# Moving two hidden-layer sums ahead of two output additions on VectorE, in six of nine blocks

## The chip, the cores and the metric

The kernel runs on one core of a Trainium2 chip. A core has a matrix engine (TensorE, PE in the profile, with its weight loads shown as PEld), a vector engine (VectorE, DVE), a scalar engine (ScalarE, ACT), a general engine (GpSimd, POOL) and a queue processor (SyncE, SP) that issues DMAs. Each engine works through its own list of instructions in order; between engines, an instruction waits on semaphores. The metric is the device time of one execution in microseconds (us), lower is better.

## What is computed

The inputs are `q`, `k`, `v` of 8 batches, 8 heads, 576 rows and 64 columns, and the weights of a two-layer network. First comes an attention in which keys and values are averaged over groups of 8 rows (72 groups), then a residual network with a mixing over rows:

```python
attn = softmax(q @ mean8(k).T / sqrt(64));  x = attn @ mean8(v)   # heads side by side: 576 x 512
u  = x + lam * (w_tok @ (alpha1 * x + beta1))                     # mixing over rows
a2 = alpha2 * u + beta2
out = u + lam * (relu(a2 @ w_ch1) @ w_ch2)                        # 512 -> 2048 -> 512
```

## The kernel before, in words

The 8 x 576 rows are cut into 36 chunks of 128 rows, and four chunks make a block, so there are nine blocks (`NBLK`), n = 0 to 8. While TensorE computes the network of block n, the attention and the row mixing of batch b = n + 1 are woven in between. The last two blocks (n = 7 and 8) have no attention beside them.

The order of the work is written out by hand. For each block, a list `todo` of pairs (place, function) is filled and sorted by place (lines 934 to 1009), and the functions are called in that order; each engine gets its own instructions in the order of the calls. A place is a number between about 0 and 31 and only orders; it is no time.

The parts that matter here, with their places in a block n = 2 to 6:

- `mlp_A(n, j)` (L651): 4 matmuls per j into a PSUM tile `ps_h` (L662), then ScalarE writes the relu as bf16 (L669) into `H4[n, j // 4]`. Sixteen j, at places 0 to 15. Each `H4` tile holds four j and 512 columns (rows of the block): the "top" columns 0 to 255 and the "low" columns 256 to 511.
- `att_AV(b, h)` (L546): five small matmuls of the attention of one head (L556, L560), then on VectorE a reciprocal (L562) and a multiplication into `x_tm` (L564). Heads 4 to 7 are at 16.5, 17.0, 18.2 and 18.7.
- `att_X` (L574) with `rest_X` (L567): two products (L578 and L571) that write `xs`, the input of the mixing. For heads 4 and 5 they are on GpSimd (17.1), for heads 6 and 7 on VectorE (18.8).
- `mix_T(b, c)` (L607): five matmuls (L614; ten half-width ones for c = 4, which exists only for odd b) at 21.0 + 1.15 c (1.3 c for b = 2), then an addition on VectorE (L618) and a cast on ScalarE (L622); 1.8 places later a DMA (L633) transposes the result into `u_fm` for the first layer of a later block.
- From the third block on (`n >= FIRST`) the second layer is done by seven products of half size instead of eight (a Strassen-like scheme). `product(n, i, pp)` (L748) is product i for half pp: 8 matmuls of 256 columns (L775). The places are 16 + 2s + pp, with i in the order 1, 2, 4, 5, 6, 3, 7. Here they are called P1 to P7.
- `hidden_sum(n, i, g)` (L734, the instruction is L744): the sums over first-layer outputs which that scheme needs, on VectorE, in bf16, 128 x 1024. g = 0 takes `H4[n, 0]` and `H4[n, 2]`, g = 1 takes `H4[n, 1]` and `H4[n, 3]`: the first and the second half of the outputs. Sum 1 adds the low columns of `hi` to those of `lo` in place; P5 reads the result, in its first four matmuls that of g = 0 and in its last four that of g = 1. Sum 2 subtracts the top columns from that and writes `S2`, which P6 and sum 4 read. Sum 4 is read by P3.
- `gather(n, i)` (L779, the instruction is L793): the output additions. It adds a finished product from PSUM to `u_sb`, on VectorE. The first waits for P1, the second for P2. P1, P6 and P7 accumulate into the same PSUM bank (called V), with additions in between; so P6 may not begin before the first addition has read V.

```python
when = ((3, (4.6, 14.6)), (1, (8.6, 19.2)), (2, (8.8, 19.4)), (4, (22.3, 23.0)))   # L965: sum i, places of g = 0, 1
order = (1, 2, 5, 6, 4, 7, 3) if last else (1, 2, 4, 5, 6, 3, 7)                   # L971
todo.append((16 + 2 * s + pp, lambda i=i, pp=pp: product(n, i, pp)))               # L974
todo.append((17.05 + 2 * s + (1.9 if i == 1 and not last else 0) + 0.01 * part,    # L976
             lambda i=i, part=part: gather(n, i, part)))
1: (lo[:, :, low], lo[:, :, low], hi[:, :, low], ALU.add),                         # L740: out, in0, in1, operation
2: (S2, lo[:, :, low], lo[:, :, top], ALU.subtract),                               # L741
nc.vector.tensor_tensor(out=o, in0=o, in1=banks[key, "both"], op=ALU.add)          # L793
```

The first output addition stands at 17.05 + 1.9 = 18.95, the second at 17.05 + 2 = 19.05. So VectorE's list in blocks n = 2 to 6 is: head 7 (L562, L564), the two products for `xs` (L578, L571), output addition 1, output addition 2, sum 1 of the second half, sum 2 of the second half, the addition of mixing 0 (L618), output addition 4 (21.05), and so on. In block n = 7 it is the same without attention and mixing. The last block (n = 8) has places of its own (L967).

Of the kernel before, what the change touches and what calls it, by code (L numbers as in the profile page):

```python
# [23 lines left out]
def kernel(  # L24
# [668 lines left out]
    def store(n, m, c0=0, c1=DM, queues=(nc.sync, nc.sync)):  # L693

        b, c = chunks[4 * n + m]
        u = u_of[n][:, m, c0:c1]
        if c < 4:
            queues[0].dma_start(
                out=out[b, 0:512, :].rearrange("(p c) d -> p c d", c=4)[:, c, c0:c1], in_=u)
        else:  # L700
            for i in range(2):
                queues[i].dma_start(out=out[b + i, 512:576, c0:c1], in_=u[64 * i:64 * i + 64, :])
# [31 lines left out]
    def hidden_sum(n, i, g):  # L734

        lo, hi, S2, S3 = H4[n, g], H4[n, g + 2], wino["S2"][g], wino["S3"][g]
        top, low = slice(0, HALF), slice(HALF, DM)
        o, a, b, op = {
            3: (S3, lo[:, :, top], lo[:, :, low], ALU.subtract),
            1: (lo[:, :, low], lo[:, :, low], hi[:, :, low], ALU.add),  # L740
            2: (S2, lo[:, :, low], lo[:, :, top], ALU.subtract),  # L741
            4: (lo[:, :, top], hi[:, :, top], S2, ALU.subtract),
        }[i]
        nc.vector.tensor_tensor(out=o, in0=a, in1=b, op=op)  # L744
# [3 lines left out]
    def product(n, i, pp):  # L748

        def stat(j):  # L750
            g, r = j // 4, j % 4
            t = {6: wino["S2"][g], 7: wino["S3"][g]}.get(i, H4[n, g + 2 * (i in (2, 4))])
            c0 = (HALF if i in (4, 5) else 0) + 128 * pp
            return t[:, r, c0:c0 + 128]

        def moving(j):
            g, r = j // 4, j % 4
            return {1: w2[g][:, r, 0:HALF], 2: w2[g + 2][:, r, 0:HALF],
                    3: w2[g + 2][:, r, HALF:], 4: w2[g][:, r, HALF:],
                    5: wino["T1"][:, j], 6: wino["T2"][g][:, r], 7: wino["T3"][:, j]}[i]  # L760

        last = n == NBLK - 1
        key = {1: "V", 6: "V", 7: "V", 2: "X", 4: "Y", 5: "Z", 3: "Z"}[i]
        first = i in (1, 2, 4, 5)
        if first and pp == 0:
            tile = (psB.tile([P, DM], FP, tag="ch", bufs=2, name="ps_w") if i < 3
                    else gp("ps_w")).rearrange("p (a d) -> p a d", a=2)
            banks[key] = [tile[:, 0], tile[:, 1]]
            banks[key, "both"] = tile
        alone = last and i == 5  # L770
        if alone and pp:
            banks[key][1] = gp("ps_w").rearrange("p (a d) -> p a d", a=2)[:, 1]
        ps = banks[key][pp]
        for j in range(8):
            nc.tensor.matmul(out=ps, lhsT=stat(j), rhs=moving(j), stop=(j == 7),  # L775
                             start=(first and (pp == 0 or alone) and j == 0),
                             skip_group_check=True)

    def gather(n, i, part=0):  # L779

        U = u_of[n]
        top, low = slice(0, 2), slice(2, 4)
        L, R = slice(0, HALF), slice(HALF, DM)
        rows, cols = {1: ((top, L),), 2: ((top, L),), 4: ((low, L),), 5: ((low, R),),
                      6: ((top, R),), 3: ((top, R),), 7: ((low, L), (low, R))}[i][part]
        key = {1: "V", 6: "V", 7: "V", 2: "X", 4: "Y", 5: "Z", 3: "Z"}[i]
        if key == "Z" and n == NBLK - 1:
            for pp in range(2):
                o = U[:, rows.start + pp, cols]
                nc.vector.tensor_tensor(out=o, in0=o, in1=banks[key][pp], op=ALU.add)  # L790
            return
        o = U[:, rows, cols]
        nc.vector.tensor_tensor(out=o, in0=o, in1=banks[key, "both"], op=ALU.add)  # L793
# [140 lines left out]
    for n in range(NBLK):  # L934
# [27 lines left out]
                todo.append((1.2 + g, lambda g=g: weight_sum(4, g)))  # L962
        if n >= FIRST:
            last = n == NBLK - 1
            when = ((3, (4.6, 14.6)), (1, (8.6, 19.2)), (2, (8.8, 19.4)), (4, (22.3, 23.0)))  # L965
            if last:
                when = ((3, (4.6, 12.6)), (1, (8.6, 16.1)), (2, (8.8, 16.2)), (4, (18.6, 19.6)))  # L967
            for i, at in when:
                for g in range(2):
                    todo.append((at[g], lambda i=i, g=g: hidden_sum(n, i, g)))  # L970
            order = (1, 2, 5, 6, 4, 7, 3) if last else (1, 2, 4, 5, 6, 3, 7)  # L971
            for s, i in enumerate(order):
                for pp in range(2):
                    todo.append((16 + 2 * s + pp, lambda i=i, pp=pp: product(n, i, pp)))  # L974
                for part in range(2 if i == 7 else 1):
                    todo.append((17.05 + 2 * s + (1.9 if i == 1 and not last else 0) + 0.01 * part,  # L976
                                 lambda i=i, part=part: gather(n, i, part)))
            if last:
                for m in range(2):
                    todo.append((19.1, lambda m=m: store(n, m, 0, HALF)))  # L980
                    todo.append((28.1, lambda m=m: store(n, 2 + m, queues=(nc.sync, nc.scalar))))
                    todo.append((29.2, lambda m=m: store(
                        n, m, HALF, DM, ((nc.sync, nc.scalar)[m],) * 2)))
            else:
                for m in range(4):
                    todo.append((27.2 if m < 2 else 29.2, lambda m=m: store(n, m)))
# [53 lines left out]
```

## Time and profile before

| | us |
|---|---|
| device time, three runs | 341.84, 343.35, 344.87 |
| their median | 343.35 |
| span of the profiled execution, first to last instruction | 339.7 |
| PE busy in that span | 328.1 (97%) |
| DVE, ACT, POOL busy | 237.3, 175.4, 94.5 |
| block n = 2 in the trace (109.0 to 144.4) | 35.4 |
| block n = 3 (144.4 to 178.3) | 33.9 |
| block n = 7 (283.0 to 309.1) | 26.1 |

For the profiled execution the page gives its span, 339.7 us, and no other time; the three runs are 2.1 to 5.2 us longer than that, the median 3.65 us. The blocks n = 2, 4, 6 have the ten half-width matmuls of a fifth mixing and are longer by 1.5 us than n = 3 and 5. Times within the trace are in us from the start of the span. Busy time of PE is not the same as PE at its peak, since matmuls overlap in the records: a 256-column matmul is listed with 0.273 us, while eight of them in a row begin 0.87 us apart from the next group, or 0.109 us each.

### The profile page before, as it was taken

The numbers are of one execution on the slowest core, as the hardware profiler recorded it, in microseconds if no ns is written. First come the engines' busy times: TensorE is split into PE (matmuls) and PEld (weight loads), VectorE is DVE, ScalarE is ACT, GpSimd is POOL, SyncE is SP. The second block draws the span as 40 slices with busy tenths as digits, with TensorE's granted clock in tenths as the row PEclk, the third lists the DMA queues.
The fourth block names the chain that finished last, engine by engine and source line by source line (L and its number), as shares of the span: only waits on it lengthen the run. The fifth ranks groups of instructions, "written<-read, shape, count | busy, mean of one in ns | idle before, by whom it ended". The sixth has DMA issues, their size and how long they took to land.

```text
span 339.7 us, 6491 instructions
## 1 busy us (share of the span) xinstructions
PE 328.1 (97%) x2524; PEld 209.0 (62%) x2524; DVE 237.3 (70%) x486; ACT 175.4 (52%) x322; POOL 94.5 (28%) x110
## 2 busy tenths in 40 slices
PE   8999999979999999999999999999999999999994
PEld 3768754435444567755775576657765766586583
DVE  7672378699779979687868787786778783263263
ACT  3767989247611880279127913583258325704800
POOL 8869352611029002710162026201420200000000
PEclk9999999998999999999999999999999999999998
DMA  8999989951996994399539943896350035003003
GB/s 123 199 212 266 268 152 267 209 132 38 159 242 116 189 168 127 70 212 181 168 69 206 198 141 68 185 188 190 49 148 2 0 53 149 0 2 125 0 31 95
DMA packets 66168, 45.81 MB, mean 135 GB/s; under 512 B 34349, under 2 KB 56501, under 8 KB 66138
## 3 DMA queue, kind: packets, MB, share of 16 engines
q1 hardware_dynamic: 51788, 32.60, 41.8%
q0 software_dynamic: 13824, 12.40, 22.5%
q10 hardware_dynamic: 526, 0.40, 0.5%
q8 instruction: 20, 0.33, 0.4%
q14 instruction: 10, 0.08, 0.1%
HBM read 38.30 MB, written 9.44 MB: 141 GB/s over the span
## 4 chain that ended last, share of the span: by engine, by line
PE 78%; DVE 15%; DMA 4%; issue 2%; POOL 0%; DVEq 0%
PE ps_h L662 30%; PE ps_w L775 21%; PE ps_tok L614 9%; PE ps_ch L682 7%; DMA v_main<-in_v_dram 4%; DVE w L710 4%; PE ps_av L556 2%; DVE u_sb L793 2%; PE ps_s L513 2%; DVE x_tm L564 2%; PE ps_warm L605 1%; DVE xs L578 1%; DVE v_u L483 1%; DVE H L744 1%; PE ps_kp L445 1%
## 5 line engine op out<-in xcount | busy, mean ns | idle before, releaser
L662 PE MATMUL ps_h<-u_fm,w 128*128 128x512 bf16 (+2 forms) x608 | 135.5, 372 | 1.3 <-DVE u_sb L689 1.0
L669 ACT ACTIVATE H<-ps_h,bias_cols 128x512 bf16<-128x512 f32 x144 | 98.1, 688 | 60.2 <-PE ps_h L662 59.2
L662 PEld LDWEIGHTS <-w 128*128 128x128 bf16 x608 | 65.8, 114 | 52.3 <-issue 5.8
L775 PEld LDWEIGHTS <-H 128*128 128x128 bf16 x560 | 53.0, 98 | 13.3 <-DVE H L744 2.6
L622 ACT CAST u_bf<-u_sb 128x512 bf16<-128x512 f32 x32 | 19.8, 618 | 73.2 <-issue 41.5
L775 PE MATMUL ps_w<-w,H 128*128 128x256 bf16 x448 | 53.8, 273 | 0.0
L793 DVE TENSOR_TENSOR u_sb<-u_sb,ps_w 128x512 f32<-128x512 f32 x54 | 36.4, 685 | 21.7 <-PE ps_w L775 21.1
L578 POOL TENSOR_TENSOR xs<-x_tm,lamal_bc 128x512 bf16<-128x512 f32 x12 | 15.1, 1266 | 110.5 <-DVE x_tm L564 110.3
L614 PE MATMUL ps_tok<-xs,wtT 128*128 128x512 bf16 (+3 forms) x200 | 44.9, 380 | 0.0
L618 DVE TENSOR_TENSOR u_sb<-x_tm,ps_tok 128x512 f32<-128x512 f32 (+1 forms) x40 | 27.4, 685 | 13.4 <-PE ps_tok L614 13.3
L564 DVE TENSOR_TENSOR x_tm<-ps_av,rec 128x320 f32<-128x320 f32 x64 | 31.5, 492 | 2.7
L542 ACT ACTIVATE ET<-ps_s 72x512 f16<-72x512 f32 x56 | 32.3, 591 | 0.0
L682 PE MATMUL ps_ch<-w,H 128*128 128x512 bf16 x128 | 30.4, 379 | 0.0
L614 PEld LDWEIGHTS <-wtT 128*128 128x128 bf16 (+3 forms) x200 | 17.4, 100 | 16.0 <-issue 1.1
L562 DVE RECIPROCAL rec<-ps_av 128x5 f32<-128x5 f32 x64 | 12.2, 191 | 17.0 <-PE ps_av L560 16.7
L483 DVE TENSOR_TENSOR v_u<-v_u 72x1024 f32<-72x1024 f32 (+1 forms) x24 | 22.8, 948 | 0.2
L775 PE MATMUL ps_w<-w_t,h_s 128*128 128x256 bf16 x168 | 22.6, 273 | 0.0
L682 PEld LDWEIGHTS <-H 128*128 128x128 bf16 x128 | 11.9, 98 | 13.7 <-issue 0.4
L185 POOL TENSOR_TENSOR k_raw<-k_raw 128x512 f32<-128x512 f32 x14 | 19.2, 1368 | 0.0
L187 POOL TENSOR_TENSOR k_bf<-k_raw 128x512 bf16<-128x512 f32 x14 | 18.8, 1342 | 1.1
L775 PEld LDWEIGHTS <-h_s 128*128 128x128 bf16 x168 | 16.4, 98 | 4.1
L744 DVE TENSOR_TENSOR h_s<-H 128x1024 bf16<-128x1024 bf16 x21 | 14.5, 690 | 6.3 <-ACT H L669 5.8
(148 smaller groups left out, 349.8 us busy)
## 6 DMA issues: line engine op xcount, KB each, us to landing
out_dram<-u_sb SPq DMA_DIRECT2D x30, 256.0 KB
k_raw<-in_k_dram SPq DMA_DIRECT2D x12, 512.0 KB
v_u<-in_v_dram SPq DMA_DIRECT2D x12, 512.0 KB
q_bf<-in_q_dram POOLq DMA_DIRECT2D x16, 256.0 KB, 6.7
w<-in_moe_w_ch_dram POOLq DMA_DIRECT2D x6, 512.0 KB, 14.2
out_dram<-u_sb SPq DMA_DIRECT2D x10, 128.0 KB
w<-in_moe_w_ch_dram POOLq DMA_DIRECT2D x1, 1024.0 KB, 14.2
k_raw<-in_k_dram POOLq DMA_DIRECT2D x2, 512.0 KB, 17.5
```

Of the source, the lines that this page charges most:

```text
L185: eng.tensor_tensor(out=raw[:, :, 0:2], in0=raw[:, :, 0:2], in1=raw[:, :, 2:4], op=ALU.add)
L483: nc.vector.tensor_tensor(out=out, in0=t[:, :, 0:width], in1=t[:, :, width:2 * width], op=ALU.add)
L542: nc.scalar.activation(out=o, in_=i, func=AF.Exp, bias=0.0, scale=0.125)
L564: nc.vector.tensor_tensor(out=x[:, 1 - odd:6 - odd, dd:dd + D], in0=av[:, :, 0:64], in1=rec.unsqueeze(2).to_broadcast((P, 5, D)), op=ALU.mult)
L614: nc.tensor.matmul(out=ps_tok[p0:p1], lhsT=wtT[0:kk, at, P * c:P * c + p1 - p0], rhs=xs_pool[i][0:kk, sc, :], start=(sc == 0), stop=(sc == 4))
L618: nc.vector.tensor_tensor(out=s["u"][p0:p1, :], in0=x[p0:p1, 1 + c if c < 4 else 5 - 5 * i, :], in1=ps_tok[p0:p1, 0:DM], op=ALU.add)
L622: nc.scalar.copy(out=s["u_bf"], in_=s["u"])
L662: nc.tensor.matmul(out=ps_h[:, t0:t1 + one], lhsT=w1_of(cc, j), rhs=rhs, start=(cc == 0), stop=(cc == 3))
L669: nc.scalar.activation(out=H4[n, j // 4][:, j % 4, :], in_=ps_h, func=AF.Relu, bias=bias_cols[:, j:j + 1], scale=1.0)
L682: nc.tensor.matmul(out=ps, lhsT=H_of(n, j)[:, 128 * m:128 * m + 128], rhs=w2[j // 4][:, j % 4, :], start=(j == 0), stop=(j == NJ - 1))
L775: nc.tensor.matmul(out=ps, lhsT=stat(j), rhs=moving(j), stop=(j == 7), start=(first and (pp == 0 or alone) and j == 0), skip_group_check=True)
L793: nc.vector.tensor_tensor(out=o, in0=o, in1=banks[key, "both"], op=ALU.add)
```

## The change

In the blocks n = 2 to 7 (the third to the eighth), sum 1 and sum 2 of the second half move from the places 19.2 and 19.4 to 18.91 and 18.92. They now stand behind the `xs` products (18.8) and ahead of output additions 1 (18.95) and 2 (19.05). The last block keeps its own line. No instruction is added, taken away or given other operands.

```diff
         if n >= FIRST:
             last = n == NBLK - 1
-            when = ((3, (4.6, 14.6)), (1, (8.6, 19.2)), (2, (8.8, 19.4)), (4, (22.3, 23.0)))
+            when = ((3, (4.6, 14.6)), (1, (8.6, 18.91)), (2, (8.8, 18.92)), (4, (22.3, 23.0)))
             if last:
                 when = ((3, (4.6, 12.6)), (1, (8.6, 16.1)), (2, (8.8, 16.2)), (4, (18.6, 19.6)))
```

## The prediction

> **What bounds the kernel now.** I read the stretches block by block first, to see which engine is full.
>
> ```profile
> core 0: us, PE busy (x) PEld busy (x) DVE busy (x) ACT busy (x) POOL busy (x), PEclk, DMA share, GB/s
> 109.00:144.40 35.40, 35.04 (x284) 23.07 (x282) 29.02 (x56) 18.18 (x33) 9.86 (x12) 1.00 0.65 133
> 144.40:178.30 33.90, 33.83 (x274) 22.71 (x273) 25.72 (x51) 17.56 (x32) 8.06 (x10) 1.00 0.78 158
> 283.00:309.10 26.10, 26.10 (x178) 18.20 (x177) 10.49 (x16) 10.99 (x16) 0.00 (x0) 1.00 0.16 46
> ```
>
> From the third block on PE is the bound: it lacks 0.36 us of its block in n = 2, 0.07 in n = 3 and nothing in n = 7, at a granted clock of 1.00. VectorE has 5 to 15 us to spare per block. So a change on VectorE can only help where PE stands and waits for it. The waits of PE and of its weight loads, from 108 us on, say where that is:
>
> ```profile
> PE ps_w L775 <- DVE H L744: 1.1, 3, 0.4
> PEld L775 <- DVE H L744: 2.6, 5, 0.6
> ```
>
> Eight entries, all in the five blocks n = 2 to 6, and L744 is the hidden sums. PE's timeline shows the place, here for n = 2:
>
> ```profile
> 131.15 1.24 PE L614 MATMUL ps_tok<-xs,wtT 128*128 128x512 bf16 x5
> 132.23 0.60 PE L775 MATMUL ps_w<-w_t,H 128*128 128x256 bf16 x4
> 133.19 0.61 PE L775 MATMUL ps_w<-w_t,H 128*128 128x256 bf16 x4 [0.36 <-DVE H L744]
> 133.64 1.24 PE L614 MATMUL ps_tok<-xs,wtT 128*128 128x512 bf16 x5
> 134.72 1.04 PE L775 MATMUL ps_w<-w_t,H 128*128 128x256 bf16 x8
> 135.59 1.24 PE L614 MATMUL ps_tok<-xs,wtT 128*128 128x512 bf16 x5
> ```
>
> P5's first half begins at 132.23, runs its four matmuls on the sum of g = 0, and then stands until 133.19 for the sum of g = 1. The chain of waits says why that sum is late:
>
> ```profile
> 130.73 0.29 DVE xs L571
> 131.02 0.03 issue
> 131.05 0.70 DVE u_sb L793
> 131.75 0.03 issue
> 131.78 0.02 DVEq L793
> 131.80 0.04 issue
> 131.84 0.69 DVE u_sb L793
> 132.53 0.61 DVE H L744
> 133.14 0.05 issue
> 133.19 0.61 PE ps_w L775 x4
> ```
>
> VectorE is busy without a gap from head 7 on, and the two output additions (L793), 1.48 us, stand directly in front of the sum that PE waits for.
>
> **The change part by part.** Nothing is added or removed: per block two sums (L744, median 0.692 us) and two additions (L793, median 0.686 us) change places on VectorE. No DMA is issued by these steps and no instruction of SP, POOL or ACT moves, so their queues keep their order.
>
> *The sums go earlier.* They will begin where addition 1 begins now: 131.05 in n = 2. Sum 1 then ends at 131.05 + 0.69 = 131.74, plus the 0.05 that PE took to go on: 131.79. PE needs it after four matmuls of P5, at 132.23 + 4 x 0.109 = 132.67. That is 0.88 us of margin. In n = 3 addition 1 stands at 166.23, so the sum is there at 166.97; PE needs it at 167.68 + 0.44 = 168.12, margin 1.15 us. The inputs are ready: the last relu (L669) began at 125.69 and took 0.68. So PE's stand at this place should vanish.
>
> *What the stand costs.* I measure it as the time from the first matmul of P5's half to the first of the mixing behind it, against the same distance for P5's other half, which waits for nothing. n = 2: 133.64 - 132.23 = 1.41 against 135.59 - 134.72 = 0.87, so 0.54. n = 3: 168.79 - 167.68 = 1.11 against 0.87, so 0.24. n = 4: 1.41, so 0.54. n = 5: 1.12, so 0.25. n = 6: 1.40, so 0.53. n = 7: PE has no stand there, so 0. Sum 2.10 us. The two waits shown above bound it: 1.1 us of idle matmul time from below, since records of matmuls overlap, and 2.6 us of idle weight-load time from above, since some idle time between loads is there without a wait. I take 2.10, the distance that really shifts what follows.
>
> [...] By weight loads the sum would be 2.6 us and the time 340.75 us. [...]
>
> *The additions go later,* by two sums: the dependent pair takes 133.17 - 132.45 = 0.72 and then 0.61 to the next start, so addition 1 begins at 131.05 + 1.33 = 132.38 and ends at 133.07; addition 2 ends at about 133.85. The addition of mixing 0 stays at 133.78, and all behind it too, because the four together take as long as before. Who waits for addition 1: P6, which accumulates into bank V. It begins at 136.45 now (its weight load) and at 135.91 after; margin 2.84 us. For addition 2's bank nobody waits until the next block's scores. The output's DMAs come at place 27.2, far behind. In n = 7 VectorE idles 3.79 us before addition 1 (298.65); the sums fit there (the last relu ends at 297.59, the two sums at about 299.06), push addition 1 to about 298.98, and P6 begins at 303.69. Cost 0.
>
> *What is late next.* With PE 0.54 us earlier: mixing 3's addition on VectorE idled 0.76 us for PE and will idle about 0.22. P3 needs sum 4, which ends at 136.86, against 140.25. The next block's first layer needs the transposed result of mixing 2 (cast done at 138.76, DMA issue 1.2 us), at 143.92. All of it holds, so each block begins earlier by what it gains, and the blocks from n = 7 on are PE alone.
>
> Sum on the profiled execution: 339.7 - 2.1 = 337.6 us of span. Against the median, 3.65 us above that span: 343.35 - 2.1 = **341.25 us** (-0.6%).
>
> **The rivals.**
>
> *A, the forecast:* the stand goes, nothing takes its place: 341.25 (1.1 to 2.6 us: 340.75 to 342.25).
>
> *B, no change, because PE runs into the next wait.* A PE that comes 0.54 us earlier could stand at the mixing behind P5, at P6, or at the block's start for something that doesn't move with it. Then 343.35. Against it: the margins above are 2.84 us and more, and no other wait of PE for a VectorE result is in this stretch. For it: the trace can't show a wait that PE's lateness hides.
>
> *C, GpSimd is held up by the sums.* Each sum reads two operands from SBUF, an addition only one. GpSimd was slower beside such VectorE work: L185 took 1.26 us at 62.93 and 1.72 at 65.49, while VectorE did products of weights (L710). The `xs` product of heads 4 and 5 on GpSimd (L578, L571), which mixing 0 needs, ends at 130.15, and at 165.55 in n = 3; the sums would begin 0.9 and 0.68 us later. It decides if GpSimd were later by more than that. By those rows it would lose 2 x 0.46 us, to 131.07, and mixing 0 begins at 131.15: no loss, 341.25 still. Held up for both sums (1.41 us) it would end at 131.56 and 166.96, mixing 0 would be late by 0.41 and 0.37, and the blocks would gain 0.13 three times and lose 0.13 twice: 343.2. [...]
>
> *D, slower: the additions hold up P6.* Place: bank V, read by addition 1, then written by P6. It begins to cost when addition 1 ends 2.84 us later than I have it, and outweighs the gain from 3.4 us. The longest idle time that VectorE has in front of an addition is 3.79 us. With that, addition 1 would end at 136.86 in n = 2 and at 172.04 in n = 3, where P6 is due at 135.91 and 171.59: with the gain set against it, 0.41 lost three times and 0.21 twice, 345.0. Against it: P1, for which that addition waits, is over before the sums begin, so nothing is there to wait for.
>
> *E, more than the stand goes:* in n = 2, 4, 6 the weight load of P3 also waits for an L793, 1.2 us in all. If the new order took that too, with 2.6 for the sums: 3.8 us, 339.55. Against it: PE's matmuls run on at that place, so little of it is time.
>
> **How the numbers follow.** A 78%, B 8%, C 4%, D 4%, E 6%. A is the likeliest, so 341.25. The three runs before are spread from 341.84 to 344.87, so a new median can be off by 1.5 us either way around a right sum: from A's 340.75 less about 1.2 to B's and C's 343.35 gives the range 339.6 to 343.4. It leaves out D, E's lower part and a wide miss. One per cent, 3.4 us, is about what a measurement of this kernel can tell from no change. Of the cases only E is faster by over 1% (339.55, bound 339.92); with 3% for the spread of runs that is 9%. Slower by over 1% (346.8) would need D at twice its price or the spread: 3%. Within 1%: 88%.
>
> **What would show it.** Right: in n = 2 to 6 P5's half is one group of eight matmuls, 0.87 us to the mixing behind it, and the waits of PE and PEld for L744 are gone; on VectorE L744 stands ahead of L793, addition 1 ends at about +2 us from the `xs` product, and the addition of mixing 0 stays where it was against its neighbours; blocks of 34.9 (n = 2, 4, 6) and 33.65 us (n = 3, 5), 26.1 in n = 7; span about 337.6. Wrong: P5 still stands for L744 (the sum waited for something); a new wait of PE for L793 at P6 (D); L578 on GpSimd longer than 1.28 us (C); blocks of the old length without that stand (B).

## The result, and the profile after

| | before | after |
|---|---|---|
| median of 20 runs, us | 343.33 | 340.62 |
| ratio after to before, 95% interval | | 0.9943 (0.9917 to 0.997) |
| span of the profiled execution, us | 339.7 | 341.0 |
| begin of the third block in it | 109.01 | 112.44 |
| from there to the end of the span | 230.7 | 228.6 |

By that ratio the kernel is faster by 0.6% (by the medians 2.71 us or 0.8%); the forecast was 341.25 us, also 0.6%. One of the 20 runs of the changed kernel took 425.35 us at a granted clock of 0.762; it counts in the median, which is 340.54 without it, and not in the ratio. The profiled execution of the changed kernel is nevertheless longer than that of the old one, 341.0 against 339.7. That is no contradiction: nothing is changed ahead of the third block, and that block begins 3.4 us later in this execution. From the third block on the changed kernel is shorter by 2.1 us. So the stretch from there to the end is the measure below (the block begins with the first line of `ps_h` matmuls in the chain of waits; the timeline, where records of matmuls overlap, lists these matmuls about 0.16 us earlier); it is the same within 0.1 us from one profile to the next, where the 20 runs of the kernel before go from 341.32 to 346.5 us.

Block by block, the first columns being the stretch and its length:

```profile
core 0: us, PE busy (x) PEld busy (x) DVE busy (x) ACT busy (x) POOL busy (x), PEclk, DMA share, GB/s
112.44:147.35 34.91, 34.75 (x280) 23.19 (x282) 28.99 (x56) 18.19 (x33) 9.37 (x11) 1.00 0.64 135
147.35:180.97 33.62, 33.41 (x269) 22.79 (x272) 25.71 (x51) 17.56 (x32) 8.33 (x10) 1.00 0.83 159
284.40:310.50 26.10, 26.00 (x176) 18.19 (x177) 10.61 (x17) 10.99 (x16) 0.00 (x0) 1.00 0.16 47
```

n = 2 went from 35.4 to 34.91 us and n = 3 from 33.9 to 33.62; n = 7 kept its 26.1. (Some matmul records are missing from this trace, 280 of 284 in the first line, so PE's busy time is a little low.) PE's timeline in n = 2:

```profile
134.57 1.24 PE L614 MATMUL ps_tok<-xs,wtT 128*128 128x512 bf16 x4
135.65 1.04 PE L775 MATMUL ps_w<-w_t,H 128*128 128x256 bf16 x8
136.53 1.24 PE L614 MATMUL ps_tok<-xs,wtT 128*128 128x512 bf16 x5
```

P5's first half is one group of eight now, and the mixing begins 0.88 us after it; it was 1.41. VectorE's timeline at the same place:

```profile
134.16 0.29 DVE L571 TENSOR_TENSOR xs<-x_tm,lamal_bc 64x128 bf16<-64x128 f32 x1
134.48 0.69 DVE L744 TENSOR_TENSOR H<-H,H 128x1024 bf16<-128x1024 bf16 x1
135.20 0.69 DVE L744 TENSOR_TENSOR h_s<-H 128x1024 bf16<-128x1024 bf16 x1
135.81 1.47 DVE L793 TENSOR_TENSOR u_sb<-u_sb,ps_w 128x512 f32<-128x512 f32 x2
137.20 0.68 DVE L618 TENSOR_TENSOR u_sb<-x_tm,ps_tok 128x512 f32<-128x512 f32 x1
...
141.71 0.69 DVE L618 TENSOR_TENSOR u_sb<-x_tm,ps_tok 128x512 f32<-128x512 f32 x1 [0.22 <-PE ps_tok L614]
```

Sum 1 ends at 135.17, 0.92 us before PE's fifth matmul of that group wants it (135.65 + 4 x 0.109 = 136.09). The additions begin 1.33 us after the sums, and the addition of mixing 0 comes 2.72 us after the first of the four; it was 2.73. All waits of the weight loads that are left from 108 us on:

```profile
PEld L513 <- issue: 2.0, 5, 0.4
PEld L662 <- issue: 1.6, 10, 0.2
PEld L775 <- DVE u_sb L793: 1.2, 3, 0.4
PEld L614 <- issue: 0.6, 3, 0.2
```

The line for L744 is gone, and PE's own list of waits in that stretch is empty.

### The profile page after: what moved, and what is told of

It is laid out like the page before. It is cut to its first block, busy times and chain, and to the rows that moved or that the text cites. A ratio compares the mean times of both kernels' runs of the same rounds, so it can differ in the third digit from the quotient of the medians.

```text
span 341.0 us, 6461 instructions
## 1 busy us (share of the span) xinstructions
PE 328.0 (96%) x2493; PEld 211.5 (62%) x2524; DVE 237.7 (70%) x486; ACT 175.6 (52%) x322; POOL 94.5 (28%) x110
## 4 chain that ended last, share of the span: by engine, by line
PE 90%; DVE 6%; issue 1%; DMA 1%; POOL 0%; DVEq 0%
PE ps_h L662 34%; PE ps_w L775 25%; PE ps_tok L614 11%; PE ps_ch L682 7%; DVE w L710 3%; PE ps_av L556 2%; PE ps_s L513 2%; PE ps_kp L445 1%; PE ps_warm L605 1%; PE ps_q L402 1%; PE ps_sc L493 1%; DMA vecs<-in_moe_lam_dram 1%; PE ps_bc L304 1%; DVE u_sb L618 1%; PE ps_r L520 1%
## 5 line engine op out<-in xcount | busy, mean ns | idle before, releaser
L793 DVE TENSOR_TENSOR u_sb<-u_sb,ps_w 128x512 f32<-128x512 f32 x54 | 36.4, 684 | 18.7 <-PE ps_w L775 18.2
L578 POOL TENSOR_TENSOR xs<-x_tm,lamal_bc 128x512 bf16<-128x512 f32 x12 | 15.2, 1266 | 110.2 <-DVE x_tm L564 110.1
L614 PE MATMUL ps_tok<-xs,wtT 128*128 128x512 bf16 (+2 forms) x193 | 44.5, 380 | 0.4
L564 DVE TENSOR_TENSOR x_tm<-ps_av,rec 128x320 f32<-128x320 f32 x64 | 31.5, 492 | 2.7
L744 DVE TENSOR_TENSOR H<-H,H 128x1024 bf16<-128x1024 bf16 x14 | 9.7, 690 | 14.3 <-ACT H L669 14.2
L185 POOL TENSOR_TENSOR k_raw<-k_raw 128x512 f32<-128x512 f32 x14 | 19.2, 1369 | 0.0
L187 POOL TENSOR_TENSOR k_bf<-k_raw 128x512 bf16<-128x512 f32 x14 | 18.8, 1340 | 1.1
```

The costliest lines, as they stand in the source:

```text
L185: eng.tensor_tensor(out=raw[:, :, 0:2], in0=raw[:, :, 0:2], in1=raw[:, :, 2:4], op=ALU.add)
L564: nc.vector.tensor_tensor(out=x[:, 1 - odd:6 - odd, dd:dd + D], in0=av[:, :, 0:64], in1=rec.unsqueeze(2).to_broadcast((P, 5, D)), op=ALU.mult)
L614: nc.tensor.matmul(out=ps_tok[p0:p1], lhsT=wtT[0:kk, at, P * c:P * c + p1 - p0], rhs=xs_pool[i][0:kk, sc, :], start=(sc == 0), stop=(sc == 4))
```

## The experiments

The theory: PE stands in five blocks for sum 1 of the second half, for nothing else, and what is behind the sums on VectorE has slack. Rivals: the gain comes from both sums or from the later additions; the earlier the sums, the better; VectorE's work counts as such; the gain is spread between runs. All numbers in one table; "stretch" is the span less the begin of the third block, and ratios are to the kernel before, run beside each kernel, with their 95% intervals. The median of that kernel was 343.33 us beside the first row of ratios, 344.89 beside the next three and "second block reordered", and 342.3 to 342.4 beside the others. So ratios of different groups don't compare to some tenths of a per cent, and the stretch is what tells these kernels apart.

| kernel | third block begins | stretch | median | ratio |
|---|---|---|---|---|
| before | 109.01 | 230.7 | | |
| after | 112.44 | 228.6 | 340.62 | 0.9943 (0.9917 to 0.997) |
| sum 1 alone ahead | 112.38 | 228.6 | 340.46 | 0.9894 (0.9831 to 0.9956) |
| sums between the additions | 108.77 | 228.6 | 339.49 | 0.9863 (0.9806 to 0.9919) |
| three blocks only | 113.62 | 229.1 | 340.18 | 0.9869 (0.9804 to 0.9935) |
| sums ahead of the xs products | 108.73 | 233.7 | 345.0 | 1.0091 (1.0049 to 1.0133) |
| one more sum ahead | 109.08 | 228.6 | 341.02 | 0.9955 (0.9914 to 0.9995) |
| two more sums ahead | 108.76 | 231.3 | 343.36 | 1.0026 (0.9999 to 1.0053) |
| addition 1 at 22.2 | 112.65 | 228.6 | 341.31 | 0.9962 (0.9927 to 0.9998) |
| addition 1 at 23.9 | 108.90 | 238.5 | 349.44 | 1.0221 (1.0176 to 1.0266) |
| sums beside GpSimd | 113.40 | 235.6 | 350.83 (one run) | |
| second block reordered | 106.54 | 228.6 | 336.95 | 0.9794 (0.9745 to 0.9842) |
| second block, last quarter later | 104.63 | 228.6 | 335.54 | 0.9808 (0.9777 to 0.984) |
| after, again | 110.50 | 228.6 | 341.14 | 0.9961 (0.9928 to 0.9995) |

**Which of the moves does it.**

```diff
-(1, (8.6, 18.91)), (2, (8.8, 18.92))
+(1, (8.6, 18.91)), (2, (8.8, 19.4))
```

> Only sum 1 of the second half stands ahead of the two output additions; sum 2 goes back behind them (19.4). Measure: the time in the trace from the first matmul of the third block to the end of the span, 230.7 us before and 228.6 after the change. Theory (PE stands in the second half of P5's first matmuls for sum 1, and for nothing else): 228.6, ratio to before 0.994. Rival (the gain comes from both sums being early, or from the additions being later): only part of it, about 229.6.

Measured: 228.6, the whole gain. Sum 2 can stay where it was; only sum 1 was waited for.

```diff
-(1, (8.6, 18.91)), (2, (8.8, 18.92))
+(1, (8.6, 18.96)), (2, (8.8, 18.97))
```

> The two sums stand between output addition 1 and output addition 2. Sum 1 then starts 0.7 us later than in the changed kernel. In the changed kernel's third block it would end at about 135.18 + 0.69 = 135.87, and PE wants it after four matmuls of P5, at 135.65 + 0.44 = 136.09: theory, no stand is left, 228.6 us from the third block to the end. Rival (the earlier the sum, the better): half of the gain, 229.6.

Measured: 228.6. On VectorE:

```profile
130.81 0.69 DVE L793 TENSOR_TENSOR u_sb<-u_sb,ps_w 128x512 f32<-128x512 f32 x1
131.41 0.69 DVE L744 TENSOR_TENSOR H<-H,H 128x1024 bf16<-128x1024 bf16 x1
```

Sum 1 ends at 132.10. P5's half begins at 131.99 and wants it at 132.43. So in this block one addition ahead is free, and two cost 0.54 us: there is a point from which the wait begins, and the stretch doesn't fall smoothly with the place of the sum.

**Where it comes from, block by block.**

```diff
-(1, (8.6, 18.91)), (2, (8.8, 18.92))
+(1, (8.6, 18.91 if n in (2, 4, 6) else 19.2)), (2, (8.8, 18.92 if n in (2, 4, 6) else 19.4))
```

> The change is made in the blocks n = 2, 4 and 6 alone; n = 3, 5 and 7 keep the old order. Theory (distance from P5's half to the mixing behind it, 0.54 us in each of these blocks and 0.24 in n = 3 and 5): gain 1.62, 230.7 - 1.6 = 229.1 us from the third block to the end. Rival (all five blocks gain alike): 1.26, 229.4. Rival (idle time of the weight loads is the size, 0.64 in each): 1.9, 228.8.

Measured: 229.1, as the distances between matmul groups said (the rivals had 229.4 and 228.8); 0.5 us is left in n = 3 and 5. The waits of the weight loads give those two blocks

```profile
PEld L775 <- DVE H L744: 0.7, 2, 0.3
```

0.7 us, which is more than they cost.

**Further ahead is worse.**

```diff
-(1, (8.6, 18.91)), (2, (8.8, 18.92))
+(1, (8.6, 18.75)), (2, (8.8, 18.76))
```

> The two sums move further ahead, in front of the two xs products of heads 6 and 7 (18.75). Theory (only what PE needs next counts): mixing 0 waits for those products, which end 1.33 us later, at 132.35 instead of 131.02 in the times of the kernel before, and mixing 0 was due at 131.15: a stand of 1.23 us in n = 2, 4, 6 and of 1.08 in n = 3 and 5, 5.9 us in all. From the third block to the end 228.6 + 5.9 = 234.5 us, ratio to before about 1.011. Rival (the earlier the sums, the better): 228.6 or less.

Measured: 233.7, so a loss of 5.1 us against the change, where 5.9 was expected. PE and then VectorE in n = 2:

```profile
128.25 2.79 PE L775 MATMUL ps_w<-w,H 128*128 128x256 bf16 x24
131.89 1.24 PE L614 MATMUL ps_tok<-xs,wtT 128*128 128x512 bf16 x5 [0.85 <-DVE xs L578]
```

```profile
129.56 0.85 DVE L744 TENSOR_TENSOR H<-H,H 128x1024 bf16<-128x1024 bf16 x1
130.45 0.69 DVE L744 TENSOR_TENSOR h_s<-H 128x1024 bf16<-128x1024 bf16 x1
131.06 0.68 DVE L578 TENSOR_TENSOR xs<-x_tm,lamal_bc 128x512 bf16<-128x512 f32 x1
131.77 0.29 DVE L571 TENSOR_TENSOR xs<-x_tm,lamal_bc 64x128 bf16<-64x128 f32 x1
```

The expectation let mixing 0 wait for L571, the smaller of the two products, but PE goes on at 131.89 while that one is still running: the first four matmuls read only what the L578 products wrote, the fifth what the L571 products wrote. L578 ends 0.32 us before L571, and PE goes on 0.15 us after that end (131.74 to 131.89), so each stand is shorter than expected by about 0.17 us. PE's 24 matmuls were through at 128.25 + 24 x 0.109 = 130.87, so it stood for 1.02 us in n = 2, and by the same count for 0.98 in n = 3: 3 x 1.02 + 2 x 0.98 = 5.0.

**How much room sum 1 has.** Each of the next two kernels repeats the subtraction of sum 3, second half, in n = 2 to 6.

```diff
+            if n < NBLK - 2:
+                for _ in range(1):     # 2 in the second kernel
+                    todo.append((18.905, lambda: hidden_sum(n, 3, 1)))
```

> The changed kernel with one more instruction on VectorE in each of the blocks n = 2 to 6: the subtraction of sum 3 of the second half is done once more, with the same result, directly ahead of sum 1. It takes 0.61 us from start to start. Theory (sum 1 has a margin of 0.88 us in n = 2, 4, 6 and 1.15 us in n = 3, 5): no cost, 228.6 us from the third block to the end. Rival (VectorE's work counts in full): 228.6 + 5 x 0.61 = 231.7.

> The same with two more instructions. Theory: 1.22 us against the margins, so sum 1 is late by 0.35 us in n = 2, 4, 6 and by 0.07 in n = 3, 5: 1.2 us in all, 229.8 us from the third block to the end. Rival (VectorE's work counts in full): 234.7.

Measured: 228.6 with one, 231.3 with two. One more sum per block on VectorE is free, as the theory has it, though it takes 0.80 us from start to start (131.11 to 131.91 in n = 2) and not 0.61. Two cost 2.7 us and not 1.2. The timeline with two, VectorE and PE in n = 2:

```profile
130.80 1.42 DVE L744 TENSOR_TENSOR w_t<-H 128x1024 bf16<-128x1024 bf16 x2
132.32 0.69 DVE L744 TENSOR_TENSOR H<-H,H 128x1024 bf16<-128x1024 bf16 x1
```

```profile
131.98 0.60 PE L775 MATMUL ps_w<-w_t,H 128*128 128x256 bf16 x4
133.07 0.61 PE L775 MATMUL ps_w<-w_t,H 128*128 128x256 bf16 x4 [0.49 <-DVE H L744]
```

The two take 132.32 - 130.80 = 1.52 us from start to start, not 1.22: they write the same tile, and sum 1 writes what they read, so each begins only when the one before has ended (the second of the two ends at 132.22, and sum 1 begins 0.10 us later). Late by 133.07 - 132.42 = 0.65 us in n = 2, and by 0.36 in n = 3 (168.36 against 168.00): 3 x 0.65 + 2 x 0.36 = 2.7.

**Who waits for addition 1.**

```diff
-todo.append((17.05 + 2 * s + (1.9 if i == 1 and not last else 0) + 0.01 * part,
+todo.append((22.2 if i == 1 and n < NBLK - 2 else     # 23.9 in the second kernel
+             17.05 + 2 * s + (1.9 if i == 1 and not last else 0) + 0.01 * part,
```

> The changed kernel with output addition 1 moved further back in n = 2 to 6, behind the addition of mixing 1 (22.2). It will run at about 138.4 to 139.1 in the times of the changed kernel, and P6, which writes the same bank, begins at 139.56. Theory (nobody waits for the addition but P6, margin about 2.8 us): no cost, 228.6 us from the third block to the end. Rival (a later output addition costs by itself): more than 228.6, up to 2 us in each block.

> The changed kernel with output addition 1 moved back to 23.9 in n = 2 to 6, directly in front of P6's place and behind the addition of mixing 2. VectorE will reach it at about 140.8 in the times of the changed kernel and end at 141.5; P6 is due at 139.56. Theory (the addition holds up P6 once it ends more than 2.8 us later than in the changed kernel): PE stands 2.0 us in each of five blocks, 228.6 + 10 = 238.6 us from the third block to the end, ratio to before about 1.023. Rival (the bank is not what P6 waits for): 228.6.

Measured: 228.6 at 22.2, 238.5 at 23.9. At 22.2, VectorE and PE in n = 2:

```profile
138.62 0.68 DVE L793 TENSOR_TENSOR u_sb<-u_sb,ps_w 128x512 f32<-128x512 f32 x1
```

```profile
139.77 1.04 PE L775 MATMUL ps_w<-w_t,h_s 128*128 128x256 bf16 x8
```

The addition ends at 139.30, and P6 begins at 139.77, unhindered. At 23.9, VectorE and PE:

```profile
137.29 0.68 DVE L793 TENSOR_TENSOR u_sb<-u_sb,ps_w 128x512 f32<-128x512 f32 x1
```

```profile
134.94 1.24 PE L614 MATMUL ps_tok<-xs,wtT 128*128 128x512 bf16 x5
138.02 1.03 PE L775 MATMUL ps_w<-w_t,h_s 128*128 128x256 bf16 x8 [1.83 <-DVE u_sb L793]
```

P6 was due at 134.94 + 1.08 = 136.02 and begins at 138.02, 0.05 us after the addition's end: 2.0 us in each of five blocks, 9.9 in all. So the mechanism of rival D is there; in the change it is 2.8 us away (addition 1 ends at 136.50, the weight load of P6 begins at 139.34).

**The sums beside GpSimd.**

```diff
-(1, (8.6, 18.91)), (2, (8.8, 18.92))
+(1, (8.6, 18.6)), (2, (8.8, 18.61))
```

> The two sums at 18.6, between the attention steps of head 6 and head 7 on VectorE, so that they run while GpSimd does its xs products of heads 4 and 5 (128.36 to 130.15 in the times of the kernel before; the sums begin at about 129.2). Theory, if the two engines do not hold each other up: the xs products on VectorE and head 7 are later by 1.33 us, mixing 0 with them, as with the sums ahead of the xs products: 234.5 us from the third block to the end, the sums 0.69 us each, GpSimd 1.27 and 0.45. [...]

Measured: 235.6, which is 1.9 us more than with the sums directly ahead of the xs products (233.7), 0.4 per block. VectorE and GpSimd in n = 2:

```profile
133.60 0.95 DVE L744 TENSOR_TENSOR H<-H,H 128x1024 bf16<-128x1024 bf16 x1
134.59 0.83 DVE L744 TENSOR_TENSOR h_s<-H 128x1024 bf16<-128x1024 bf16 x1
```

```profile
132.74 1.26 POOL L578 TENSOR_TENSOR xs<-x_tm,lamal_bc 128x512 bf16<-128x512 f32 x1 [17.86 <-DVE x_tm L564]
134.08 0.79 POOL L571 TENSOR_TENSOR xs<-x_tm,lamal_bc 64x128 bf16<-64x128 f32 x1
```

The sums take 0.95 and 0.83 us instead of 0.69, and GpSimd's second product 0.79 instead of 0.45, while its first, which was running already, keeps its 1.26. So in this run the two do hold each other up when they meet, and the one that comes second loses the time of the meeting, but for about 0.14 us: sum 1 met GpSimd's first product for 0.40 us and lost 0.26, GpSimd's second product then met sum 1 for 0.47 and lost 0.34, and sum 2 met that product for 0.28 and lost 0.14. In n = 3 the same three met for 0.46, 0.58 and 0.28 us and lost 0.33, 0.44 and 0.14.

The 0.4 us per block against the other kernel is not all of it this meeting. There, too, sum 1 met GpSimd's second product (129.42 to 129.87) and took 0.85 us instead of 0.69, so the meetings cost VectorE 0.40 us here and 0.16 there in n = 2, or 0.24 more. Another 0.13 is that head 7's L564 now stands directly in front of L578, which reads its result and starts 0.53 us after it, where sum 1 started 0.40 us after it.

**The same reading one block earlier.** The changed kernel has such stands in its second block (n = 1) too. The waits of PE there:

```profile
PE ps_s L513 <- DVE kp L457: 2.1, 1, 2.1
PE ps_kp L445 <- DVE u_sb L689: 1.5, 1, 1.5
```

```diff
-            for piece in range(8):
+            for piece in range(2):
                 at = 27.3 + 0.55 * piece
...
-            for piece in range(8):
-                todo.append((1.0 + 1.7 * piece, lambda k=piece: scale_w2(2 + k // 4, k % 4)))
+            for piece in range(2, 16):
+                at = 4.2 + 1.3 * (piece - 2) if piece < 8 else 12.0 + 0.95 * (piece - 8)
+                todo.append((at, lambda k=piece: scale_w2(k // 4, k % 4)))
```

> The same reading one block earlier, on top of the change. In the second block (n = 1) of the changed kernel PE stands 1.50 us at 77.17 for an output addition (L689) and 2.15 us at 81.54 for the copy of the averaged keys (L457); VectorE's list has multiplications of second-layer weights (L710) in front of both, which are needed much later. Six of eight of them that stand at the end of the first block, and the eight of the second block, move behind the keys' copy and spread to place 18.65. Theory (PE stands for what VectorE does first in its list): the two stands go, up to 3.65 us, so a ratio to before near 0.994 - 0.011 = 0.983; the stretch from the third block to the end stays 228.6. Rival (VectorE has no slack in the second block, so the multiplications only delay the next thing PE needs): no gain over the changed kernel, ratio 0.994.

Measured: 336.95 us, against 339.49 to 340.46 for the three kernels with the gain or most of it that ran beside it. Both stands are gone, and a new one is there:

```profile
PE ps_tok L614 <- DVE xs L578: 1.8, 1, 1.8
```

So less came of it than the 3.65 us. Between the first transpose of the mixing weights (L329) and the third block lie 106.54 - 18.26 = 88.3 us, against 108.77 - 17.88 = 90.9 with the sums between the additions, an execution with a like start: 2.6 us. PE's waits between 25 and 108 us add up to 5.6 us in that execution and to 3.1 here, which is 2.5 less. The rival was half right: the moved multiplications delayed the next thing that PE needed. The last multiplications then moved once more:

```diff
-                at = 4.2 + 1.3 * (piece - 2) if piece < 8 else 12.0 + 0.95 * (piece - 8)
+                at = (4.2 + 1.3 * (piece - 2) if piece < 8 else
+                      12.0 + 1.2 * (piece - 8) if piece < 12 else 18.9 + 0.01 * piece)
```

> On top of the kernel that moves weight multiplications in the second block. There one stand was new: mixing 0 waited 1.82 us at 93.41 for the xs products of VectorE (L578), which stood behind the last multiplications (L710, places 12 to 18.65). Those of the last quarter of w2, which PE needs last, now stand behind the xs products (19.0 to 19.1). Theory (what stands ahead of the needed instruction is paid for, what stands behind it is not): the stand goes, about 1.8 us less than that kernel, near 0.975 of the time before; from the third block to the end 228.6 us. Rival (VectorE's total work in the second block is the limit): the stand moves to the addition of mixing 0 or to the second layer, no gain.

> The changed kernel once more, on the same chip as the kernel above, for the comparison. Theory: 0.994 of the time before, 228.6 us from the third block to the end, whatever the time at which the third block begins. Rival (the gain lies in the early part and is spread of runs): another length of that stretch, and a ratio that follows the start.

Measured: 335.54 us, against 341.14 for the changed kernel beside it. The stand for L578 is gone, 104.63 - 18.02 = 86.6 us of early part, 1.7 less, so VectorE's total work was not the limit; PE's longest wait from 60 us on is

```profile
PE ps_h L662 <- DMA u_fm<-u_bf: 0.5, 1, 0.5
```

This version beats both kernels: ratio 0.9808 (0.9777 to 0.984) to the kernel before, where the change alone had 0.9961 (0.9928 to 0.9995) beside it.

## Why the prediction was right, point by point

- *The sums go earlier, PE's stand vanishes.* Shown. The margin in n = 2 was put at 0.88 us, with 0.05 for PE to go on; counted in the same way it is 0.87. One more sum fits into it, two don't. That it is sum 1 and nothing else is shown by sum 1 alone giving all of it.
- *The size, 2.10 us by the distance between matmul groups.* Shown: 230.7 - 228.6 = 2.1, and 0.5 of it in n = 3 and 5. The bounds on either side, 1.1 from idle matmul time and 2.6 from idle weight loads, held as bounds, but neither is the size: the weight loads were idle for 0.7 us in two blocks that lose 0.5. Here the distance of the matmuls' starts was better than both.
- *The additions go later at no cost.* Shown. Addition 1 begins 1.33 us after the sums begin, as worked out, and even 2.6 us later (138.62 instead of 136.01 in that kernel) it costs nothing. In n = 7 it begins 15.91 us after the block instead of 15.60, 0.31 later; 0.33 was forecast, and the block has its old length.
- *What is late next.* Mixing 3's addition idles 0.22 us, as worked out. No wait took the old one's place, so rival B is out.
- *Rival C* needs the two engines to meet, and in the change they don't: GpSimd's second product ends at 133.58 in n = 2, the sums begin at 134.48. In the run that makes them meet, the one that comes second loses the time of the meeting less about 0.14 us: GpSimd's second product lost 0.34 us in n = 2 and 0.44 in n = 3 and its first nothing, where the rows gave 0.46 for each. No run shows a GpSimd held up for both sums, the 1.41 us that the 343.2 of this rival rests on; that was the author's estimate.
- *Rival D* exists as a mechanism and is 2.8 us away. *Rival E* is out: the wait of P3's weight load for L793 is listed unchanged, 1.2 us, three times.
- *The step that was loose* is the 3.65 us between the profiled span and the median. It was treated as one number, but it is mostly spread: the profiled run of after took 342.73 us with a span of 341.0, so about 1.7 lie around the span, and the profiled execution of before was one of the shorter ones of its kernel. The forecast didn't suffer, as a difference was taken from the median. That the new median lies within 0.6 us of the forecast is in part luck, since the median of the kernel before alone was between 342.32 and 344.89 us from one group of runs to the next. What bears the forecast out is the stretch, 2.1 us.
- *A misreading without effect:* VectorE was said to have 5 to 15 us to spare per block; the rows give 6.4, 8.2 and 15.6.

## What to carry to other kernels

Where one engine is full, look at what stands in front of the instruction that it waits for in the other engine's list; the sum that is needed first goes first, but only behind what is needed earlier still: sums ahead of products that PE needed sooner cost 5.1 us here, sums behind two additions that could wait 2.1. Size a stand by the distance between the starts of the full engine's groups, against the same group without a wait. And when runs differ by more than the gain, measure from a place in the trace behind the part that differs.

## What the runs showed of the hardware

Most of the spread between the profiled executions is made in the first 20 us, by the matrix engine's speed. The same eight transposes (L402) in the early part, in the profiled execution of before and then of after:

```profile
13.49 0.61 PE L402 MATMUL ps_q<-identity_bf,q_bf 128*128 128x128 bf16 x8
```

```profile
15.77 1.01 PE L402 MATMUL ps_q<-identity_bf,q_bf 128*128 128x128 bf16 x8
```

From the start of these eight to that of the next group it is 0.44 us in before (13.49 to 13.93) and 0.80 in after (15.77 to 16.57). In after, matmuls run at about half speed until 17 us, in before until 10 (eight of them took 0.83 us at 6.27). The granted clock is listed as 1.00 in both at that time, so only the matmuls' own times show it. The transposes of the mixing weights then begin at 17.85 and 20.65, and the third block at 109.01 and 112.44. Of the 14 profiles five (after, and the kernels whose third block begins at 112.38, 112.65, 113.40 and 113.62) are the late case, with those transposes at 20.6 to 21.8, and nine the early one, 17.7 to 18.3. The kernel doesn't decide it: the code up to there is the same in all, and the changed kernel has both, since those transposes begin at 18.30 in "after, again". The end of the slow stretch differs by 7 us between before and after, and that costs 2.8 us by the begin of the transposes of the mixing weights, more than the change gives.

A smaller part comes later. In the second block, where PE stands, the granted clock falls to 0.50 in some executions. The changed kernel, and then the one with the sums between the additions, which doesn't show it (columns as above, the clock is the third from the end):

```profile
83.00:85.00 2.00, 1.91 (x5) 0.73 (x5) 1.86 (x8) 0.98 (x3) 0.49 (x1) 0.50 0.00 0
```

```profile
83.00:85.00 2.00, 2.00 (x11) 1.00 (x9) 1.86 (x6) 2.00 (x4) 0.33 (x1) 1.00 0.65 194
```

The kernel before has it from 75 to 77 us, and "after, again" from 81 to 83. From the first of those transposes to the third block it is 90.9 us without it, and 91.2 (before), 91.8 (after) and 92.2 (after, again) with it. From the third block on the granted clock was 1.00 in the blocks shown.

On VectorE, in the profiles of before and after, from the third block on, an instruction that doesn't wait for another engine starts 0.59 to 0.62 us after a sum or an addition of 0.67 to 0.70 us that it is independent of (only the memset L168 starts 0.02 to 0.03 us after one). When it isn't, it starts 0.71 to 0.73 us after (sum 2 behind sum 1), and in the runs with repeated sums 0.80 (sum 1 behind the repeated sum 3). The prediction had the first two from its rows; the third made the two repeated sums dearer than expected.
